# A new written order of one core's instruction queues up to the fifth token group, in a kernel of local attention and a softplus feed-forward layer

## The chip, the cores and the metric

The kernel runs on one core of one Trainium2 chip. The metric is the device time of one execution in microseconds. A core has five engines with a queue each: TensorE (PE; its weight loads are shown as PEld), VectorE (DVE), ScalarE (ACT), GpSimd (POOL) and SyncE (SP, which here only issues transfers). Each queue runs in the order in which it was written, and an instruction that has to wait holds up everything behind it in its queue.

## The reference

Attention over 4 sequences, 8 heads, 768 positions and 64 channels, with a window of the last 96 positions, the first 8 positions for all, and a bias by distance; then two matrix products with a softplus between them.

```python
scores = scale * np.matmul(q, k.transpose(0, 1, 3, 2))
...
scores = scores + bias[None, :, :, :]
scores = np.where(keep, scores, -1000000000.0)
...
a = np.exp(scores)
a = a / (np.sum(a, axis=-1, keepdims=True) + 1e-09)
return np.matmul(a, v).astype(np.float32)
...
h = x @ w_in
g = np.maximum(h, 0.0) + np.log1p(np.exp(-np.abs(h)))
return (g @ w_out).astype(np.float32)
```

x is the attention's output as 3072 tokens of 512 channels; w_in is 512 x 2048, w_out 2048 x 512.

## The kernel before, in words

The tokens are worked in 24 blocks of 128 (`blocks`, line 286), two blocks to a unit (12 units, `UNITS`, line 147) and two to a group of the feed-forward layer (12 groups). Every piece of work is an operation with a name, made by `op` (line 28) with what it reads and writes; `ORDER` (lines 68 to 145) lists the names of all 1045 operations with the engine of each (P, V, A, G, S), and `in_order` (line 56) emits them in that order, so the order of every queue is written out by hand. An operation that can run on several engines (its `alts`) runs on the one that `ORDER` names. The waits follow from what each operation reads and writes. The numbers in a name are the group, block or unit, then the part.

Attention, for unit i or block n:

- `ldq`, `ldk`, `ldv` (line 569): transfers of q, k, v of a unit from DRAM into one of 14 raw tiles, issued by SP (`ldq0.0` and `ldq0.1` by ACT). From unit 3 on they also wait for a given product of the feed-forward layer (`gates`, line 1337).
- `castq`, `castk`, `castv` (lines 650, 682, 690): to bf16.
- `trq`, `trk`: transposes, for units 0 to 2 on PE (line 777) with the evictions `cpq`, `cpk` on DVE or ACT, from unit 3 on by DMA, issued by SP (line 823).
- `gk`, `gv` (lines 846, 862): copies of the 8 global positions into the neighbour block's keys and values.
- `sc` (line 918; `sb` puts the bias into PSUM for blocks 0 and 1), `z` (line 978, adds the bias on DVE), `ex` (line 987, the exponential on ACT), `pv` (line 1009), `nm` (line 1021, reciprocal and multiply on DVE).
- `xt` (line 1023): the transposed attention output into the tile XT; for blocks 0 to 5 on PE with the eviction `xc`, from block 6 on by DMA, issued by SP. The row `PE x_ps L1002` is pv, `s_ps L950` sc, `XT<-xs` xt.

Feed-forward layer, for group g:

- `win`, `wout` (line 617): eight transfers of 512 KB each for w_in and for w_out, cast by `cin` and `cout` (line 644).
- `a{g}.{p}` (line 1069): eight matmuls (row `h_ps L1060`) into one of two PSUM banks; needs both blocks' XT and two slices of w_in. `e` (line 1081) is the exponential on ACT, `ln` (line 1093) the logarithm over two `e`.
- Groups 0 and 1: `b{g}.{ns}.{x}` (line 1122), two matmuls of 512 columns each (row L1107), as the slices of w_out come in; `oc` and `st` (line 1126) copy and store.
- Groups 2 to 11: the second product in the form with seven instead of eight block products. `ws` (line 396) makes sums of w_out's blocks, `ka` (line 438) those of the activations, `b{g}.{j}` (line 525) the products (row L522), `oe` the sums into the output tile, `st` the stores (line 550).

`fill` are matmuls on a zero tile at the start. `iota`, `dl`, `d0`, `bias`, `ident`, `ident_q`, `ident_p`, `ones`, `table` (lines 1148 to 1230) make the constants; `table` loads ACT's function table (line 344). `castk3.0`, for example, is unit 3's k, and `pv5.1` block 5's second half of the heads.

What sets the order around the change: the first units' q, k and v, then w_in, then w_out come through SP's one queue; the products of groups 0 and 1 are interleaved with them slice by slice; in between, the attention of blocks 4 to 9 makes the XT tiles for groups 2 to 4. `pv` of blocks 4 and later writes the bank x_ps, so each needs the `nm` of the one before.

Of the kernel before, what the change touches and what calls it, by code (L numbers as in the profile page):

```python
# [73 lines left out]
win0:S castq0.1:V fill15:P fill16:P win1:S cpq0.0:V trq0.1:P cpk0.0:V castk0.1:A cpq0.1:V sc0.0:P biasTrue5:A
ident_p:V sb1.0:P biasTrue6:V ex0.0:A win3:S trk0.1:P sb1.1:P ex0.1:A cpk0.1:V castk1.0:V sc1.1:P win2:S castq1.1:V
sc1.0:P ex1.1:A castq1.0:V fill17:P castk1.1:G fill18:P fill19:P pv0.0:P fill20:P ex1.0:A nm0.0:V fill21:P castv0.11:G
trk1.0:P ldq2.0:S fill22:P castv1.11:G cpk1.1:V pv0.1:P pv1.1:P nm0.1:V trq1.0:P cpk1.0:A ldq2.1:S castv1.00:G
fill23:P nm1.1:V cpq1.0:A xt0:P ldk2.1:S pv1.0:P castv1.01:A fill24:P cpq1.1:V fill25:P win5:S fill26:P cin0:G nm1.0:V
xc0:A win4:S sc2.0:P xt1:P z2.0:V win6:S fill27:P castk2.0:G xc1:A fill28:P z2.1:V sc3.0:P gk4:A gv4.1:G ex2.0:A
fill29:P cin1:V sc3.1:P castv1.10:A win7:S pv2.0:P fill30:P z3.0:V cin3:G ex2.1:A fill31:P a0.1:P wout0:S nm2.0:V  # L80
a0.0:P ex3.0:A cin2:V wout1:S pv2.1:P fill32:P e0.0:A nm2.1:V fill33:P fill34:P wout2:S castq2.0:A z3.1:V a0.2:P
castq2.1:A ldv2:S e0.1:A xt2:P castk2.1:G trq2.0:P xc2:V ex3.1:A wout3:S gv4.0:G trk2.0:P cpq2.1:V a0.3:P cin5:G
cpq2.0:A cpk2.0:V cpk2.1:V e0.2:A pv3.0:P e0.3:A cin4:G sc4.0:P nm3.0:V ln0.0:A z4.1:V pv3.1:P gk5:G a0.5:P ln0.1:A
# [1305 lines left out]
```

## Time and profile before

| | |
|---|---|
| three runs | 210.63, 210.78, 211.83 us (median 210.78) |
| the profiled execution | 210.41 us, of it the span from first to last instruction 208.6 us |
| granted TensorE clock | 1.0 over the whole span |
| busy in the span | PE 200.5, PEld 164.2, DVE 160.1, ACT 169.2, POOL 114.1 us |
| from HBM, to HBM | 27.26 MB, 6.29 MB |

In the profile's lines, L and a number is a line of the kernel. A line of the timeline has the start and the duration in us, the engine (SPq is a transfer that SP issues), the line, the operation, out<-in by the names of the tiles, shapes, the count of merged instructions, and in brackets the idle time of the engine before it with what ended it. Ends of matmuls are modelled: consecutive ones overlap, so the time that one holds PE is read from start to start. A few matmul records are missing. The chain of work that ended last is given as start, duration, and what. A table of stretches gives, for each, the busy time of every engine and in brackets the instructions, then the granted clock, the busy share of the DMA engines, and GB/s.

### The profile page before, as it was taken

The numbers are of one execution on the slowest core, as the hardware profiler recorded it, in microseconds if no ns is written. First come the engines' busy times: TensorE is split into PE (matmuls) and PEld (weight loads), VectorE is DVE, ScalarE is ACT, GpSimd is POOL, SyncE is SP. The second block draws the span as 40 slices with busy tenths as digits, with TensorE's granted clock in tenths as the row PEclk, the third lists the DMA queues.
The fourth block names the chain that finished last, engine by engine and source line by source line (L and its number), as shares of the span: only waits on it lengthen the run. The fifth ranks groups of instructions, "written<-read, shape, count | busy, mean of one in ns | idle before, by whom it ended". The sixth has DMA issues, their size and how long they took to land.

```text
span 208.6 us, 5507 instructions
## 1 busy us (share of the span) xinstructions
PE 200.5 (96%) x2202; PEld 164.2 (79%) x2211; DVE 160.1 (77%) x297; ACT 169.2 (81%) x246; POOL 114.1 (55%) x120
## 2 busy tenths in 40 slices
...
GB/s 176 364 361 388 387 358 361 335 227 255 210 218 282 187 207 286 191 236 300 195 191 259 209 194 214 159 133 126 104 75 54 100 5 138 66 0 0 104 21 181
DMA packets 70649, 40.99 MB, mean 196 GB/s; under 512 B 30432, under 2 KB 62688, under 8 KB 70624
## 3 DMA queue, kind: packets, MB, share of 16 engines
...
q10 hardware_dynamic: 688, 0.66, 1.0%
...
HBM read 27.26 MB, written 6.29 MB: 161 GB/s over the span
## 4 chain that ended last, share of the span: by engine, by line
PE 73%; DMA 14%; DVE 4%; ACT 2%; POOL 2%; issue 1%; SPq 1%; ACTq 0%; POOLq 0%; DVEq 0%
PE h_ps L1060 35%; PE o_ps L522 25%; DMA raw<-in_q_dram 7%; DMA raw<-in_moe_w_in_dram 5%; PE x_ps L1002 4%; PE s_ps L950 4%; DMA XT<-xs 2%; PE x_ps L522 2%; PE s_ps L1107 2%; PE s_ps L522 1%; POOL vb L868 1%; SPq L640 1%; DVE z L976 1%; POOL qb L675 1%; ACT g L1086 1%
## 5 line engine op out<-in xcount | busy, mean ns | idle before, releaser
L1060 PE MATMUL h_ps<-XT,w_in_bf 128*128 128x256 bf16 x768 | 94.8, 273 | 2.1 <-DMA XT<-xs 1.2
L1060 PEld LDWEIGHTS <-w_in_bf 128*128 128x128 bf16 x768 | 73.2, 98 | 13.4 <-DMA XT<-xs 1.4
L1075 ACT ACTIVATE e<-h_ps 128x512 f32<-128x512 f32 x96 | 60.0, 637 | 16.8 <-PE h_ps L1060 16.1
L1086 ACT ACTIVATE g<-e 128x1024 bf16<-128x1024 f32 x48 | 49.5, 1051 | 0.4
L976 DVE TENSOR_TENSOR z<-s_ps,biasA 128x1024 f32<-128x1024 f32 x38 | 45.9, 1218 | 4.0 <-PE s_ps L950 2.7
L983 ACT ACTIVATE pb<-z 128x1024 bf16<-128x1024 f32 (+1 forms) x44 | 43.5, 992 | 2.4 <-DVE z L976 1.7
L452 POOL TENSOR_TENSOR g<-g 128x1024 bf16<-128x1024 bf16 x12 | 26.0, 2168 | 23.1 <-DVE raw L452 22.9
L522 PEld LDWEIGHTS <-g 128*128 128x128 bf16 x320 | 30.8, 98 | 3.6
L452 POOL TENSOR_TENSOR raw<-g 128x1024 bf16<-128x1024 bf16 x9 | 19.9, 2214 | 15.2 <-ACT g L1086 13.6
L522 PEld LDWEIGHTS <-raw 128*128 128x128 bf16 x240 | 22.5, 98 | 2.8
L522 PE MATMUL o_ps<-raw,raw 128*128 128x256 bf16 x192 | 24.3, 273 | 0.0
L452 DVE TENSOR_TENSOR raw<-g 128x1024 bf16<-128x1024 bf16 x21 | 17.3, 833 | 6.7 <-ACT g L1086 4.2
L522 PE MATMUL o_ps<-raw,g 128*128 128x256 bf16 x160 | 19.7, 273 | 0.0
L868 POOL COPY vb<-vb 4x512 bf16<-4x512 bf16 x22 | 15.2, 692 | 6.8 <-PE x_ps L1002 6.0
L1002 PEld LDWEIGHTS <-pb 128*128 128x128 bf16 x352 | 16.4, 98 | 3.0 <-issue 0.3
L1014 DVE TENSOR_TENSOR xs<-x_ps,rcp 128x256 bf16<-128x256 f32 x40 | 17.0, 425 | 1.4
L707 POOL CAST vb<-raw 64x512 bf16<-64x512 f32 x26 | 16.5, 640 | 2.7 <-DMA raw<-in_v_dram 1.5
L1002 PE MATMUL x_ps<-vb,pb 128*128 128x65 bf16 x304 | 15.8, 193 | 0.1
L522 PE MATMUL o_ps<-w_out_bf,g 128*128 128x256 bf16 x128 | 15.8, 273 | 0.0
L1013 DVE RECIPROCAL rcp<-x_ps 128x4 f32<-128x4 f32 x40 | 7.1, 178 | 7.2 <-PE x_ps L1002 6.5
L1234 PE MATMUL x_ps<-blank 128*128 128x512 bf16 x32 | 11.0, 454 | 1.5 <-DVE blank L1159 1.2
L675 POOL CAST qb<-raw 128x1024 bf16<-128x1024 f32 x7 | 8.1, 1152 | 7.4 <-DMA raw<-in_q_dram 7.1
...
## 6 DMA issues: line engine op xcount, KB each, us to landing
...
```

What stands on the lines that cost most here:

```text
L452: (nc.vector if eng == "DVE" else nc.gpsimd).tensor_tensor(dst, a[0], b[0], ALU.subtract)
L522: nc.tensor.matmul(psum(j), lhs[:, f // 2, f % 2, :], w(f), start=(f == 0 and not (chain and j in "267")), stop=(f == 7), skip_group_check ...
L707: copy_on[eng](dst, src)
L868: copy_on[eng](vb_of(prev)[sl, :, 0:D], vb_of(first)[sl, :, 0:D])
L976: nc.vector.tensor_tensor(z, src, bias, ALU.add)
L983: nc.scalar.activation(pb[:, 0:nr, :].rearrange("p (y a) b -> p y (a b)", y=2), src, AF.Exp, scale=1.0 / root_d)
L1002: nc.tensor.matmul(xv[:, h, :], pb[:, 4 * (h % 2) + 2 * part + h // 2 if lone else u_all * (2 * (h % 2) + h // 2) + u, :], vb_of(prev if u ...
L1014: nc.vector.tensor_tensor(xs[:, 4 * part : 4 * part + 4, :], xv[:, :, 0:D], rcp[:][:, :, None].to_broadcast([P, 4, D]), ALU.mult,)
L1060: last = nc.tensor.matmul(hv[:, j, :], w_in_bf[:, m, fb * P : fb * P + P], XT[g % NXG][:, m, :], start=(m == 0), stop=(m == NM - 1),)
L1075: nc.scalar.activation(e[:, p % 2, :, :].rearrange("p j (b t r) -> p (j b) r t", b=2, r=2), hb[:].rearrange("p (a r t) -> p a r t", a=4, r=2),
L1086: nc.scalar.activation(gt[:, 2 * p - 2 : 2 * p + 2, :].rearrange("p a t -> p (a t)"), e[:].rearrange("p a j t -> p (a j t)"), AF.Ln, bias=1.0,
L1234: nc.tensor.matmul(x_ps[:], blank[:, 0:P], blank[:])
```

## The change

Only `ORDER` changes. The same 1045 operations are there; 82 of them have another engine: 20 go from ACT to DVE, 17 from POOL to DVE, 16 from DVE to POOL, 16 from DVE to ACT, 8 from POOL to ACT and 5 from ACT to POOL. The last 277 entries of the list are as before, and so are the last 155 of PE's 324 entries (from b3.3 on), 114 of DVE's, 123 of ACT's, 50 of POOL's and 52 of SP's. Core of the diff:

```diff
 ENGINES = {"P": "PE", "V": "DVE", "A": "ACT", "G": "POOL", "S": "SP"}
 ORDER = """
-ldv0:S iota:G ldq0.0:A blank:V fill0:P ldk0.0:S ldq0.1:A dl0a:V fill1:P dl0b:V ldk0.1:S fill2:P table:A dl0c:V dl1a:V
-fill3:P fill4:P ldk1.0:S fill5:P d0:G d0e:V fill6:P ldq1.0:S fill7:P dl1c:V biasFalse4:G biasFalse1:A ldq1.1:S fill8:P
...
-cin6:G z4.0:V a0.4:P e0.5:A cin7:G nm3.1:V wout4:S ex4.0:A sc5.0:P xt3:P gv8.0:G a0.7:P e0.4:A z5.1:V cout0:G wout5:S
-xc3:A a0.6:P e0.7:A z5.0:V cout1:G ex4.1:A a1.1:P ldq3:S ws0.4:V ldk3:S e0.6:A b0.0.0:P cout2:G gk6:A b0.1.0:P ws0.3:V
-e1.1:A a1.0:P ex5.0:A a1.3:P castv2.11:V ln0.2:A wout7:S ws0.1:V b0.0.2:P ws0.6:V b0.1.2:P e1.0:A b0.0.4:P castv2.01:V
-castv2.00:A cout3:V a1.2:P ln1.0:A cout4:G pv4.0:P b0.1.4:P e1.2:A nm4.0:V b0.0.6:P ln0.3:A gk8:G ws1.3:V b0.1.6:P
-wout6:S pv4.1:P e1.3:A ldv3:S a1.4:P nm4.1:V gv5.1:G ws1.6:V b0.0.8:P e1.4:A xt4:P ws1.4:V b1.0.0:P gv5.0:A cout5:V
-b1.0.2:P ex5.1:A a1.5:P ws0.7:V xc4:A castv2.10:V b0.1.8:P castq3.0:V ln1.1:A b0.1.10:P ws1.7:V b0.0.10:P trq3:S
-cout7:G e1.5:A pv5.0:P a1.6:P castk3.0:A nm5.0:V ldq4:S ws2.3:V b1.0.4:P e1.6:A trk3.0:S pv5.1:P b1.0.6:P cout6:A
...
-e2.2:A ldk5:S pv6.1:P a2.4:P nm6.1:V gv7.0:G ex7.0:A gv7.1:V castv4.00:G xt6:S b1.1.0:P z7.1:V e2.3:A b1.1.2:P e2.4:A
-b1.1.4:P castv3.11:V trk4.1:S a2.5:P ex7.1:A castq5.0:V pv7.0:P ln2.0:A b1.1.6:P st0.0.0:S nm7.0:V sc8.0:P trq5:S
-ws3.4:V ln2.1:A castk5.0:G pv7.1:P a2.6:P nm7.1:V e2.5:A z8.0:V xt7:S b1.1.8:P gk9:A ws3.3:G e2.6:A b1.1.10:P ln2.2:A
...
+ldv0:S iota:G table:A ldq0.0:A blank:V fill0:P ldk0.0:S ldq0.1:A ones:G dl0a:V fill1:P dl0b:V ldk0.1:S ident:G dl1a:V
+fill2:P dl0c:V dl1c:V fill3:P d0:G fill4:P d0e:V ldk1.0:S fill5:P dl1e:V biasFalse7:G fill6:P ldq1.0:S biasTrue2:V
...
+z4.0:V a0.5:P cin7:G a0.4:P wout6:S nm3.1:V e0.5:A z4.1:V gk5:A xt3:P ex4.0:A cout0:G a0.7:P wout7:S xc3:V e0.4:A
+wout5:S sc5.0:P ws0.6:V e0.7:A ldq3:S a0.6:P z5.1:V cout1:A ldk3:S a1.1:P gk6:V e0.6:A gv8.1:V cout2:V b0.1.0:P
+ln0.2:A a1.0:P ws0.3:V e1.1:A castv2.01:G z5.0:V b0.1.2:P castv2.00:A a1.3:P e1.0:A ws0.4:V castv2.10:A pv4.0:P ldv3:S
+ws0.7:V b0.0.0:P e1.3:A b0.1.4:P nm4.0:V ex4.1:A a1.2:P ws1.4:V cout3:V b0.0.2:P e1.2:A pv4.1:P a1.5:P ln0.3:A nm4.1:V
+ws1.1:V b0.0.4:P ln1.1:A b0.0.6:P ws0.1:V a1.4:P e1.5:A cout4:V ex5.0:A ws1.7:V xt4:P b0.0.8:P cout5:V b0.1.6:P
+ln1.0:A a1.7:P ws1.3:V cout6:V cout7:A ldk4:S b0.1.8:P castv2.11:V b0.0.10:P xc4:V castq3.0:A b0.1.10:P gv5.1:V
+gv8.0:V b0.0.12:P ws2.1:V gv5.0:A b1.0.0:P trq3:S ws2.7:V ex5.1:A b1.0.2:P pv5.0:P castk3.0:V b0.0.14:P e1.4:A ws2.3:V
+b1.0.4:P trk3.0:S castv3.10:G b0.1.12:P ln1.2:A nm5.0:V b0.1.14:P castv3.00:V ws2.4:G pv5.1:P ldq4:S a1.6:P nm5.1:V
...
+ex6.1:A nm6.0:V a2.3:P ldv4:S z7.0:V ldk5:S pv6.1:P e2.3:A b1.1.0:P gv7.0:G a2.4:P nm6.1:V ex7.0:A castq5.0:G z7.1:V
+a2.5:P ln2.1:A gv7.1:G trq5:S b1.1.2:P e2.4:A pv7.0:P sc8.0:P e2.5:A nm7.0:V xt6:S castv4.01:G b1.1.4:P ex7.1:A z8.0:V
+b1.1.6:P castv4.00:G b1.1.8:P ln2.0:A gk9:G castv4.11:V pv7.1:P a2.7:P nm7.1:V castk5.0:G ex8.0:A z8.1:V a2.6:P xt7:S
...
```

The queues that result, in the stretch that matters, old and then new.

PE, from a0.5 to group 3's first product:

```
a0.5 a0.4 sc5.0 xt3 a0.7 a0.6 a1.1 b0.0.0 b0.1.0 a1.0 a1.3 b0.0.2 b0.1.2 b0.0.4 a1.2 pv4.0 b0.1.4 b0.0.6 b0.1.6 pv4.1 a1.4 b0.0.8 xt4 b1.0.0 b1.0.2 a1.5 b0.1.8 b0.1.10 b0.0.10 pv5.0 a1.6 b1.0.4 pv5.1 b1.0.6 a1.7 xt5 b0.0.12 b0.1.12 b0.1.14 b0.0.14 a2.0 b1.0.8 b1.0.10 sc6.0 b1.0.12 b1.0.14 a2.1 a2.2 pv6.0 sc7.0 a2.3 pv6.1 a2.4 b1.1.0 b1.1.2 b1.1.4 a2.5 pv7.0 b1.1.6 sc8.0 pv7.1 a2.6 b1.1.8 b1.1.10 b1.1.12 a2.7 b1.1.14 sc9.0 a3.0

a0.5 a0.4 xt3 a0.7 sc5.0 a0.6 a1.1 b0.1.0 a1.0 b0.1.2 a1.3 pv4.0 b0.0.0 b0.1.4 a1.2 b0.0.2 pv4.1 a1.5 b0.0.4 b0.0.6 a1.4 xt4 b0.0.8 b0.1.6 a1.7 b0.1.8 b0.0.10 b0.1.10 b0.0.12 b1.0.0 b1.0.2 pv5.0 b0.0.14 b1.0.4 b0.1.12 b0.1.14 pv5.1 a1.6 xt5 b1.0.6 b1.0.8 a2.0 sc6.0 a2.1 b1.0.10 b1.0.12 a2.2 b1.0.14 pv6.0 sc7.0 a2.3 pv6.1 b1.1.0 a2.4 a2.5 b1.1.2 pv7.0 sc8.0 b1.1.4 b1.1.6 b1.1.8 pv7.1 a2.7 a2.6 pv8.0 b1.1.10 sc9.0 b1.1.12 b1.1.14 pv8.1 a3.1
```

SP, from the fourth slice of w_out on:

```
wout3 wout4 wout5 ldq3 ldk3 wout7 wout6 ldv3 trq3 ldq4 trk3.0 ldk4 trk3.1 ldv4 trq4 ldq5 trk4.0 ldk5 xt6 trk4.1 st0.0.0 trq5 xt7 st0.1.0 ldv5 ldq6 trk5.0 ldk6 xt8 ldv6 trk5.1 xt9

wout3 wout4 wout6 wout7 wout5 ldq3 ldk3 ldv3 ldk4 trq3 trk3.0 ldq4 trk3.1 ldq5 trk4.1 trk4.0 trq4 ldv4 ldk5 trq5 xt6 xt7 st0.0.0 st0.1.0 ldk6 trk5.0 ldv5 trk5.1 ldv6 ldq6 xt8 xt9
```

DVE, from z5.1 to z6.0:

```
z5.1 z5.0 ws0.4 ws0.3 castv2.11 ws0.1 ws0.6 castv2.01 cout3 nm4.0 ws1.3 nm4.1 ws1.6 ws1.4 cout5 ws0.7 castv2.10 castq3.0 ws1.7 nm5.0 ws2.3 nm5.1 gv6.0 ws2.6 ws1.1 ws2.4 ws3.6 ws2.1 oc0.0.0 ws2.7 z6.0

z5.1 gk6 gv8.1 cout2 ws0.3 z5.0 ws0.4 ws0.7 nm4.0 ws1.4 cout3 nm4.1 ws1.1 ws0.1 cout4 ws1.7 cout5 ws1.3 cout6 castv2.11 xc4 gv5.1 gv8.0 ws2.1 ws2.7 castk3.0 ws2.3 nm5.0 castv3.00 nm5.1 oc0.1.0 xc5 ws2.6 ws1.6 gv6.1 castk4.0 z6.0
```

POOL, from cout0 to castk5.0:

```
cout0 cout1 cout2 cout4 gk8 gv5.1 cout7 castq4.0 gv8.1 castv3.00 gv6.1 castk4.0 ws3.1 gv7.0 castv4.00 castk5.0

cout0 castv2.01 castv3.10 ws2.4 castv3.11 castq4.0 ws3.1 ws3.6 gv7.0 castq5.0 gv7.1 castv4.01 castv4.00 gk9 castk5.0
```

ACT, in the same stretch, now has cout1, castv2.10, cout7, castq3.0, gv6.0 and oc0.0.0, and no longer gk6, xc4, castk3.0, cout6, xc5, oc0.1.0 and castv3.10. POOL's cin5 is now followed by gk8 before cin4.

127 lines of the change are left out of this document (63 added, 64 removed).

## The prediction

> **What bounds the kernel now.** I read the page's busy times first, then stretches of the span, then TensorE's and the other queues' timelines around each place where TensorE stops, and last the chain that ended last. In the page PE is the fullest engine; in the table of stretches (span from 0) its busy time against the length of the stretch tells where it stops.
>
> ```profile
> span 208.6 us, 5507 instructions
> ...
> PE 200.5 (96%) x2202; PEld 164.2 (79%) x2211; DVE 160.1 (77%) x297; ACT 169.2 (81%) x246; POOL 114.1 (55%) x120
> ```
>
> ```profile
> core 0: us, PE busy (x) PEld busy (x) DVE busy (x) ACT busy (x) POOL busy (x), PEclk, DMA share, GB/s
> 0.00:17.30 17.30, 15.52 (x153) 8.46 (x156) 13.35 (x43) 12.21 (x25) 7.46 (x18) 1.00 0.93 309
> 17.30:28.50 11.20, 10.06 (x127) 7.90 (x127) 9.04 (x18) 10.06 (x15) 6.45 (x8) 1.00 1.05 387
> 28.50:50.00 21.50, 21.34 (x190) 14.85 (x192) 20.50 (x35) 20.77 (x33) 8.91 (x11) 1.00 1.08 305
> 50.00:64.74 14.74, 13.26 (x153) 9.51 (x155) 13.76 (x21) 13.38 (x21) 9.54 (x12) 1.00 1.21 223
> 64.74:202.45 137.71, 137.71 (x1562) 121.38 (x1563) 100.60 (x177) 112.83 (x156) 81.76 (x74) 1.00 0.69 148
> ```
>
> From 64.74 us on, when the third group's first product a3.0 begins, PE is busy without a gap, at the full granted clock. So the end is fixed by when a3.0 starts. Up to 28.5 us the DMA engines are full (387 GB/s) and the slices of w_in come one by one: POOL's timeline shows the last four casts (cin5, cin4, cin6, cin7) each waiting for its landing, 1.35 us apart.
>
> ```profile
> 23.47 1.04 POOL L644 CAST w_in_bf<-raw 128x1024 bf16<-128x1024 f32 x1 [0.18 <-DMA raw<-in_moe_w_in_dram]
> 27.53 1.04 POOL L644 CAST w_in_bf<-raw 128x1024 bf16<-128x1024 f32 x1 [0.31 <-DMA raw<-in_moe_w_in_dram]
> ```
>
> PE's timeline gives the other two marks. In the written order its rows are a0.7, a0.6 and a1.1 at 28.57, right behind cin7; then sc6.0 (49.26), a2.5 (56.62), pv7.0 (57.73), b1.1.6 (57.97), sc9.0 (62.88) and a3.0 with a3.1 (64.74).
>
> ```profile
> 28.57 2.86 PE L1060 MATMUL h_ps<-XT,w_in_bf 128*128 128x256 bf16 x24
> ...
> 49.26 0.62 PE L950 MATMUL s_ps<-qT,kT 64*128 64x128 bf16 x16
> ...
> 56.62 1.04 PE L1060 MATMUL h_ps<-XT,w_in_bf 128*128 128x256 bf16 x8
> 57.73 0.40 PE L1002 MATMUL x_ps<-vb,pb 128*128 128x65 bf16 x8
> 57.97 0.59 PE L1107 MATMUL o_ps<-w_out_bf,g 128*128 128x512 bf16 x2
> ...
> 62.88 0.62 PE L950 MATMUL s_ps<-qT,kT 64*128 64x128 bf16 x16
> 64.74 1.92 PE L1060 MATMUL h_ps<-XT,w_in_bf 128*128 128x256 bf16 x16 [1.24 <-DMA XT<-xs]
> ```
>
> How long an operation holds PE is read from the chain, which counts from one start to the next: 0.87 for an a, 0.43 for a b of two matmuls (1.29 for three), 0.24 for a pv, 0.55 for a wide sc, and on DVE 1.13 for a z; for an xt I take 0.22 (four of the same 0.055).
>
> ```profile
> 21.30 1.13 DVE z L976
> ...
> 34.04 1.29 PE s_ps L1107 x6
> ...
> 60.53 4.17 DMA XT<-xs
> 64.74 1.92 PE h_ps L1060 x16
> 66.66 0.24 PE x_ps L1002 x8
> 66.90 0.87 PE o_ps L522 x8
> ...
> 72.87 0.55 PE s_ps L950 x16
> ```
>
> From a0.7 (28.57) to a3.0 (64.74) are 36.17 us. The written order has there 18 a (two of group 0, eight each of 1 and 2), 32 small b, 8 pv, 2 xt and 4 wide sc: 18 x 0.8725 + 32 x 0.43 + 8 x 0.24 + 2 x 0.22 + 4 x 0.555 = 34.05. So PE waits 2.1 us in all there. The largest piece is before a3.0: sc9.0 is done at 62.88 + 0.55 = 63.43, a3.0 comes 1.3 later, when xt7's transposed tile lands. Another is 0.24 before pv7.0 (56.62 + 0.87 = 57.49 against 57.73); pv7.0 waits for castv3.11, which DVE's queue reaches only at 57.25 (its timeline).
>
> ```profile
> 57.25 0.43 DVE L707 CAST vb<-raw 64x512 bf16<-64x512 f32 x1
> ```
>
> **The change part by part.** No operation is added or removed; 82 change their engine, and every queue is reordered up to about the fourth group's work; the last 155 of PE's 324 entries stand as before.
>
> *The start.* ACT's table load comes ahead of the two ldq0 issues, which costs them between 0 and its 1.3 us; castk0.1, castq1.0, castq1.1 and ident_p go to POOL, four evictions (cpq0.0, cpk0.1, cpq1.1, cpk1.1) to ACT, one (cpq1.0) back to DVE. Worked down by hand with the rows' durations, block 1's transposed tile is late by 0 to 1 us.
>
> ```profile
> L344 ACT ACT_TABLE_LOAD x1 | 1.3, 1283 | 2.1 <-issue 2.1
> 20.05 0.69 DVE L644 CAST w_in_bf<-raw 128x1024 bf16<-128x1024 f32 x1 [0.99 <-DMA raw<-in_moe_w_in_dram]
> ```
>
> The cover is the transfer of the fourth w_in slice: cin2 cannot start before 20.05, on DVE before and on ACT now (about 1.02 instead of 0.69), so the second pair of products starts at 21.1 instead of 20.8. That 0.3, and the 0.2 that gk8 between cin5 and cin4 adds, are hidden again by cin7's landing. Value 0; without that cover, up to 1 us.
>
> *At cin7.* Before, sc5.0 ran ahead of a0.7, in the time that PE would have waited for cin7. Now it stands behind a0.7. Likewise pv8.0 and pv8.1 now stand ahead of group 3's first product. So between a0.7 and that product lie 34.05 + 0.555 + 0.48 = 35.09 us of work, of which the 0.48 was to be done later anyway. If no wait at all were left, group 3 would start at 28.57 + 35.09 = 63.66, worth 63.18 in the old order: 1.55 us are to be had (2.1 less sc5.0), not more. What is given back:
>
> *DVE between z5.1 and nm5.0.* DVE now has all of cout2 to cout6 (cout3 and cout5 were its own), castk3.0, gv8.0, gv8.1, gv5.1, xc4 and gk6, and has given castq3.0, castv2.01, castv2.10, ws2.4 and ws3.6 away. In the old order DVE was busy for 20.50 of the 21.50 us in that stretch. Its rows (and one of POOL's) give 0.60 from start to start for a weight sum, and I take the same for a cast of that size, when POOL is still; an nm holds it for 0.56 (42.90 to 43.46).
>
> ```profile
> 42.90 0.18 DVE L1013 RECIPROCAL rcp<-x_ps 128x4 f32<-128x4 f32 x1
> ...
> 43.46 0.82 DVE L417 TENSOR_TENSOR raw<-raw,raw 128x512 bf16<-128x512 f32 x1
> ...
> 46.95 0.67 DVE L417 TENSOR_TENSOR raw<-raw 128x512 bf16<-128x512 f32 x1
> 47.55 0.67 DVE L417 TENSOR_TENSOR raw<-raw,raw 128x512 bf16<-128x512 f32 x1
> ...
> 48.75 1.12 DVE L417 TENSOR_TENSOR raw<-raw 128x512 bf16<-128x512 f32 x1
> ```
>
> ```profile
> 48.29 1.04 POOL L675 CAST qb<-raw 128x1024 bf16<-128x1024 f32 x1 [4.55 <-DMA raw<-in_q_dram]
> ```
>
> sc5.0 ends at 28.57 + 0.87 + 0.56 = 30.0. Behind it DVE has 2 z (1.13), 11 ws, 5 casts and castk3.0 (17 x 0.60), 2 nm (0.56) and six small copies (1.7, an estimate from the 0.43 of the cast above): 15.3, so nm5.0 begins at 45.3 and ends at 45.9, or 46.3 where nm4.1 and cout5 wait for pv4.1 and their slice. PE reaches pv5.1, which needs the bank that nm5.0 frees, after 9 a, 19 b, 3 pv, xt4 and sc5.0, 17.5 us, at 46.1. With castv3.10 and ws2.4 on POOL at that moment it is worse, since the row at 48.75 shows a weight sum of 1.12 instead of 0.67 beside a POOL cast. I take 0.4 (0 to 1.2).
>
> The Trainium skill says why, in its page "GPSIMD Engine Reference", section "1. Specifications": POOL's SBUF interfaces are shared with VectorE, and they contend when DVE runs a two-port mode or has two SBUF inputs. The rows at 48.29 and 48.75 agree. It speaks against this change, which puts five POOL operations beside five such DVE ones; by it the wait is nearer its upper end, and the total 0.8 later than with the lower one.
>
> *SP's queue.* wout6, wout7 and wout5 now go ahead of ldq3 and ldk3, and ldk4 ahead of trq3. While the DMA engines are full, a later place is a later landing: two 512 KB slices, 1.35 each, so ldq3 and ldk3 land some 2.7 later.
>
> ```profile
> 33.90 3.98 SPq L640 DMA_DIRECT2D raw<-in_moe_w_out_dram  x2
> ...
> 42.27 1.34 SPq L837 DMA_TRANSPOSE qT<-qb  x1
> ...
> 44.33 1.38 SPq L830 DMA_TRANSPOSE kT<-kb  x1
> ```
>
> ```profile
> 42.89 1.02 ACT L687 CAST kb<-raw 128x1024 bf16<-128x1024 f32 x1
> ```
>
> ```profile
> kT<-kb SPq DMA_TRANSPOSE x8, 4.9
> ```
>
> castk3.0 on DVE ends about 45.2 (before: 43.9, on ACT), trk3.0 is issued then instead of at 44.33, and its tile lands by the listing of DMA issues 4.9 us later in the middle (at most 4.9 for this one, as sc6.0 at 49.26 needs it): 49.5 to 50.3. PE comes to sc6.0 after 11 a, 21 b, 4 pv, 2 xt and sc5.0, 20.6 us, at 49.2 plus the wait above. I take 0.3 (0 to 0.9).
>
> *Before group 3.* castv3.11 is on POOL, early, so the 0.24 before pv7.0 goes. xt7 needs nm7.1, which needs pv7.1. In the new order pv7.1 ends 4.07 us of PE work ahead of a3.1 (two a, two pv, three b, sc9.0). The chain is nm7.1 with its queue (0.75) and a transpose through DMA. The view of the XT tile gives 2.4 to 5.1 for that, 3.6 in the middle.
>
> ```profile
> DMA to landing us min/median/max: 2.4/3.6/5.1
> ```
>
> With 0.2 for issue the chain is 4.5 against 4.07 of cover: 0.45 of the old 1.3 stays (0 to 1.2, the upper end with the 4.17 of the old xt7). castq5.0 on POOL and trq5 stand ahead of xt7 on SP; by the rows they end about 58, ahead of nm7.1 at 60.9, and cost nothing unless 2 us late.
>
> *Group 4's first product.* nm9.1 now stands behind z10.0 and z10.1 on DVE; 2.4 us behind sc10.0 instead of directly behind pv9.1, so xt9 is some 0.4 later against the same products. I take 0.2 (0 to 1.0).
>
> **The sum.** -1.55 + 0.4 + 0.3 + 0.45 + 0.2 = -0.2. The profiled execution took 210.41 (span 208.6 and 1.8 around it), so it would be 210.2. The runs shown have a median of 210.78, 0.37 over the profiled one; I put half of that on top and predict 210.4.
>
> **The rivals.** *All waits go.* Nothing comes in place of the old ones: 210.41 - 1.55 = 208.9. For it: each of the four waits has 0 as its lower end. Against: all four would have to be at it, and xt7's needs a transpose faster than the middle one.
>
> *The w_in slices land earlier.* POOL's cast at 18.80 waited 1.96 for its slice, while later slices come every 1.35; had that one come on the same step, all landings behind it would be up to 1.5 us earlier, and the mark at 28.57 with them: 210.2 - 1.5 = 208.7; with some of the other waits gone too, 208.6. ldq2.0, which waited for castv0.11 in the old order, is free sooner now. Against: seven transfers were still outstanding then, so the queue was not empty.
>
> ```profile
> 18.80 1.04 POOL L644 CAST w_in_bf<-raw 128x1024 bf16<-128x1024 f32 x1 [1.96 <-DMA raw<-in_moe_w_in_dram]
> ```
>
> *Slower: DVE's queue becomes the bound from 30 to 50 us.* Its five operations beside POOL's at 45 to 48 (ws2.1, ws2.7, castk3.0, ws2.3, castv3.00) each take up to 0.45 more (1.12 against 0.67), 2 us in all. Then pv5.1 waits 1.6, trk3.0 goes out 1.4 later and sc6.0 waits 1.0, and castk4.0, trk4.0 and trq4 behind them make sc8.0 and xt7 late by 1.2 each: -1.55 + 5.0 = +3.4, 213.8 at worst, about 213.0 with two thirds of it. It decides once nm5.0 ends more than 1.5 us behind PE's arrival at pv5.1, that is after 47.6. For it: DVE has no slack there. Against: POOL's rows in that stretch sum to 8.91 of 21.50, most of them not beside these.
>
> **How the numbers follow.** The likeliest, waits that move, gets 0.66; all waits gone 0.12; slices earlier 0.06; DVE the bound 0.16. A measurement of this kernel can tell about 1% (2.1 us) from no change. The likeliest lies within it with its own range (209.0 to 212.0), and so does nearly half of "all gone", whose 208.9 is at the edge. So faster by over 1% gets 0.12, within 1% 0.72, slower 0.16. The range runs from the slices' 208.6 to 212.6, which leaves out the upper part of "DVE the bound".
>
> **What would show it.** Right: a0.7 within 0.4 of 28.57, right behind cin7; pv7.0 without a wait of its own; PE's largest gap still before group 3's first a, ended by an XT transpose, but under 1.3; a gap at pv5.1 ended by DVE's multiply. PE gapless afterwards up to group 4, and its last part as before. Wrong: a0.7 over 1 us from there (the start is not hidden), gaps over 1 us between 30 and 50, or a new gap after 70.

## The result and the profile after

The changed kernel takes 212.35 us (median of 10 runs, 211.86 to 213.34), the kernel before beside it 211.11 (10 runs): a ratio of 1.0065 (95%: 1.0045 to 1.0086). Measured again later on another chip it was 1.0092 (1.0073 to 1.0111). So it is 1.2 to 1.8 us slower, where 0.4 us faster was forecast: inside the range and within the 1%, but on the other side. The profiled execution took 212.53. Of e17, below, only two of six executions ran at a granted clock of 0.999 (the others at 0.983 to 0.992), and only those two times are used; its trace is of one of the others, with a clock of 1.00 up to 54.5 us.

The page of the changed kernel, and the table of stretches for it, cut at a0.7, a2.0, group 3's first product (now a3.1) and a4.0 (at their first weight loads):

```profile
span 210.7 us, 5495 instructions
...
PE 201.0 (95%) x2203; PEld 164.3 (78%) x2211; DVE 159.7 (76%) x300; ACT 170.4 (81%) x246; POOL 108.7 (52%) x117
```

```profile
29.06:49.36 20.30, 19.81 (x179) 13.68 (x180) 19.65 (x40) 19.54 (x28) 5.39 (x5) 1.00 1.03 291
49.36:66.75 17.39, 15.98 (x197) 11.67 (x198) 15.16 (x25) 16.47 (x23) 11.15 (x15) 1.00 1.09 197
66.75:80.86 14.11, 13.62 (x160) 11.67 (x161) 12.15 (x19) 11.55 (x20) 8.83 (x9) 1.00 1.19 228
```

The same table of before, cut at the same products:

```profile
28.52:47.22 18.70, 18.54 (x161) 13.10 (x162) 17.73 (x31) 18.00 (x28) 7.24 (x9) 1.00 1.09 312
47.22:64.74 17.52, 16.04 (x183) 11.24 (x185) 16.54 (x25) 16.12 (x26) 11.19 (x13) 1.00 1.19 229
64.74:78.38 13.64, 13.64 (x168) 12.03 (x169) 11.01 (x22) 12.38 (x18) 9.17 (x10) 1.00 1.08 222
```

PE's busy time counts overlapped ends, so the lengths of the stretches are what to compare, and the two orders put different products into them. The work moved is taken out with the durations of the prediction: in the first stretch the new order does sc5.0 (0.555) and one small b (0.43) more, in the second one b less and pv8.0 and pv8.1 (0.48) more, in the third those two less and pv10.0 (0.24) more. What is left is waiting:

| stretch | before | after | waits added | forecast |
|---|---|---|---|---|
| up to a0.7 | 28.52 | 29.06 | +0.54 | 0 |
| a0.7 to a2.0 | 18.70 | 20.30 | +0.61 | +0.4 (pv5.1) |
| a2.0 to group 3 | 17.52 | 17.39 | -0.18 | -1.35 |
| group 3 to a4.0 | 13.64 | 14.11 | +0.71 | +0.2 |
| sum of the waits | | | +1.68 | -0.75 |

With sc5.0's 0.555 and pv10.0's 0.24 that makes the 2.48 by which a4.0 comes later (80.86 against 78.38). Weight loads run a little ahead of their matmuls (pv8.1's start at 64.88, its matmuls at 65.09). Cut at the matmuls' own starts, the four rows are +0.54, +0.56, -0.11 and +0.81, together 1.80, and a4.0 comes 2.59 later; the single waits below are read from matmul to matmul. The forecast's -1.35 is its 2.1 of old waits less the 0.3 at sc6.0 and the 0.45 before a3.1. Behind a4.0 nothing more is lost: PE's last product starts 2.34 later than before (PE's order is the same from a4.6 on). This is one traced execution of each kernel, 2.12 apart in time; the medians are only 1.2 to 1.8 apart.

Where the waits sit, in the timeline of the changed kernel. At the start (a line is start, duration, engine, line, operation), first the one row of before, the eviction xc1 that finishes block 1's tile:

```profile
15.67 0.59 ACT L1038 COPY XT<-o_ps 128x512 bf16<-128x512 bf16 x1 [0.24 <-PE o_ps L1033]
```

```profile
16.33 0.60 ACT L817 COPY kTa<-s_ps 128x512 bf16<-128x512 bf16 x1
...
17.04 0.41 PE L950 MATMUL s_ps<-qT,kTa 64*128 64x128 bf16 x8 [0.59 <-ACT kTa L817]
...
18.04 0.39 PE L1033 MATMUL o_ps<-ident,xs 128*128 128x128 bf16 x4
...
18.46 0.59 ACT L1038 COPY XT<-o_ps 128x512 bf16<-128x512 bf16 x1 [1.54 <-PE o_ps L1033]
...
21.20 1.04 ACT L644 CAST w_in_bf<-raw 128x1024 bf16<-128x1024 f32 x1
...
22.29 0.94 PE L1060 MATMUL h_ps<-XT,w_in_bf 128*128 128x256 bf16 x7 [0.50 <-ACT w_in_bf L644]
```

sc2.0 (17.04) waits for cpk1.1, an eviction that ACT now reaches only at 16.33; xt1 stands behind it, so block 1's tile is done at 19.05 (before: 16.25). cin2 starts at 21.20, not when its slice lands (20.15), since e0.1 and ex2.1 stand ahead of it on ACT and wait for a0.1. From there PE is behind: a0.7 comes after a0.5, a0.4 and xt3, not right behind cin7 (28.70).

In the second stretch DVE runs without a gap from z5.1 (30.83) to nm5.0, and pv5.1 waits 0.49 for it:

```profile
45.41 0.68 DVE L687 CAST kb<-raw 128x1024 bf16<-128x1024 f32 x1
45.42 1.74 POOL L707 CAST vb<-raw 64x512 bf16<-64x512 f32 x1 [11.21 <-DMA raw<-in_v_dram]
...
46.01 0.67 DVE L417 TENSOR_TENSOR raw<-raw,raw 128x512 bf16<-128x512 f32 x1
...
46.81 0.42 DVE L1014 TENSOR_TENSOR xs<-x_ps,rcp 128x256 bf16<-128x256 f32 x1
...
47.29 0.40 PE L1002 MATMUL x_ps<-vb,pb 128*128 128x65 bf16 x8 [0.33 <-DVE xs L1014]
```

Before group 3:

```profile
56.39 0.57 SPq L609 DMA_DIRECT2D raw<-in_v_dram  x1
...
57.91 3.17 SPq L837 DMA_TRANSPOSE qT<-qb  x1
...
60.91 0.41 PE L1002 MATMUL x_ps<-vb,pb 128*128 128x65 bf16 x8
...
61.18 2.53 SPq L1045 DMA_TRANSPOSE XT<-xs  x2
61.23 0.43 DVE L707 CAST vb<-raw 64x512 bf16<-64x512 f32 x1 [0.30 <-DMA raw<-in_v_dram]
...
61.68 0.18 DVE L1013 RECIPROCAL rcp<-x_ps 128x4 f32<-128x4 f32 x1
61.90 0.42 DVE L1014 TENSOR_TENSOR xs<-x_ps,rcp 128x256 bf16<-128x256 f32 x1
...
65.09 0.41 PE L1002 MATMUL x_ps<-vb,pb 128*128 128x65 bf16 x8
...
66.76 1.48 PE L1060 MATMUL h_ps<-XT,w_in_bf 128*128 128x256 bf16 x12 [1.26 <-DMA XT<-xs]
```

ldv4 is issued at 56.39 (before: 48.37), castv4.11 waits for it on DVE until 61.20, and nm7.1 (61.68 to 62.33) stands behind castv4.11. xt7 is sent at 62.49 and lands at 66.71, 4.2 later. From pv8.1's start (65.09) to a3.1's (66.76) are 1.67, 1.43 of them a wait (before, behind sc9.0: 1.31).

And in group 3, castv5.00 waits on ACT for ldv5 (sent at 68.44, before at 63.03), and e3.5 and e3.4 stand behind it. They empty the two banks that a3.7 and a3.6 write, so PE waits 0.23 at a3.7 (76.00) and 0.57 at a3.6 (77.45):

```profile
68.44 0.56 SPq L609 DMA_DIRECT2D raw<-in_v_dram  x1
...
73.86 0.62 ACT L707 CAST vb<-raw 64x512 bf16<-64x512 f32 x1 [1.02 <-DMA raw<-in_v_dram]
...
75.35 0.60 ACT L1075 ACTIVATE e<-h_ps 128x512 f32<-128x512 f32 x1
...
76.00 1.03 PE L1060 MATMUL h_ps<-XT,w_in_bf 128*128 128x256 bf16 x8
...
76.79 0.61 ACT L1075 ACTIVATE e<-h_ps 128x512 f32<-128x512 f32 x1
...
77.45 1.03 PE L1060 MATMUL h_ps<-XT,w_in_bf 128*128 128x256 bf16 x8 [0.41 <-ACT e L1075]
```

Before, castv5.00 stood behind e3.5 and e3.4 and did not wait:

```profile
71.95 1.35 ACT L1075 ACTIVATE e<-h_ps 128x512 f32<-128x512 f32 x2
73.18 0.60 ACT L707 CAST vb<-raw 64x512 bf16<-64x512 f32 x1
```

xt9 lands at 80.34 in the changed kernel, 0.6 ahead of a4.0's matmuls, so a4.0 has no wait of its own.

### The profile page after: what moved, and what is told of

Its sections match the earlier page's. It is cut to its first block, busy times and chain, and to the rows that moved or that the text cites. A ratio compares the mean times of both kernels' runs of the same rounds, so it can differ in the third digit from the quotient of the medians.

```text
span 210.7 us, 5495 instructions
## 1 busy us (share of the span) xinstructions
PE 201.0 (95%) x2203; PEld 164.3 (78%) x2211; DVE 159.7 (76%) x300; ACT 170.4 (81%) x246; POOL 108.7 (52%) x117
## 4 chain that ended last, share of the span: by engine, by line
PE 69%; DVE 8%; DMA 7%; POOL 5%; ACT 5%; issue 3%; SPq 1%; POOLq 0%; DVEq 0%
PE h_ps L1060 31%; PE o_ps L522 24%; PE s_ps L950 4%; PE x_ps L1002 3%; POOL raw L417 3%; DMA raw<-in_v_dram 3%; DMA raw<-in_k_dram 3%; DMA raw<-in_q_dram 2%; DVE raw L417 2%; PE x_ps L522 2%; PE s_ps L522 1%; ACT pb L983 1%; PE s_ps L1107 1%; ACT g L1086 1%; ACT e L1075 1%
## 5 line engine op out<-in xcount | busy, mean ns | idle before, releaser
L452 POOL TENSOR_TENSOR g<-g 128x1024 bf16<-128x1024 bf16 x11 | 23.9, 2172 | 24.5 <-DVE raw L452 21.3
L707 POOL CAST vb<-raw 64x512 bf16<-64x512 f32 x25 | 18.2, 729 | 19.9 <-DMA raw<-in_v_dram 18.9
L452 POOL TENSOR_TENSOR raw<-g 128x1024 bf16<-128x1024 bf16 x8 | 17.5, 2187 | 16.4 <-ACT g L1086 13.8
L1002 PE MATMUL x_ps<-vb,pb 128*128 128x65 bf16 x304 | 15.8, 193 | 0.3 <-DVE xs L1014 0.3
L522 PE MATMUL o_ps<-w_out_bf,g 128*128 128x256 bf16 x128 | 15.8, 273 | 0.0
L868 POOL COPY vb<-vb 4x512 bf16<-4x512 bf16 x18 | 11.5, 640 | 6.6 <-PE x_ps L1002 6.0
L675 POOL CAST qb<-raw 128x1024 bf16<-128x1024 f32 (+1 forms) x9 | 9.3, 1031 | 6.5 <-DMA raw<-in_q_dram 6.3
L1234 PE MATMUL x_ps<-blank 128*128 128x512 bf16 x33 | 10.5, 438 | 1.3 <-DVE blank L1159 1.2
```

The lines of the kernel that those rows point to most:

```text
L452: (nc.vector if eng == "DVE" else nc.gpsimd).tensor_tensor(dst, a[0], b[0], ALU.subtract)
L522: nc.tensor.matmul(psum(j), lhs[:, f // 2, f % 2, :], w(f), start=(f == 0 and not (chain and j in "267")), stop=(f == 7), skip_group_check ...
L707: copy_on[eng](dst, src)
L868: copy_on[eng](vb_of(prev)[sl, :, 0:D], vb_of(first)[sl, :, 0:D])
L1002: nc.tensor.matmul(xv[:, h, :], pb[:, 4 * (h % 2) + 2 * part + h // 2 if lone else u_all * (2 * (h % 2) + h // 2) + u, :], vb_of(prev if u ...
```

## The experiments

All kernels ran beside the kernel before on the same chip; "+1.20" is the difference of the two medians in us, and in brackets stands the interval of the ratio. The changed kernel itself was +1.24 the first time and +1.81 (e5) the second; a0.7 lies between 28.73 and 29.10 in nine traces of the new start, and between 28.24 and 28.59 in nine of the old one, so 0.44 later in the mean (28.88 against 28.44).

**Start or rest: e1, e2, e5, e7.** The list is cut at a0.7: one order up to there, the other for what remains.

```diff
 e1: -changed order up to sc5.0        +order of before up to a0.7
 e2: -order of before up to a0.7       +changed order up to sc5.0, then before's
 e7: e1, and  -ws0.6:V e0.7:A ldq3:S a0.6:P z5.1:V   +z5.1:V ws0.6:V e0.7:A ldq3:S a0.6:P
```

> The list of before up to a0.7 (with its engines), then the remaining operations in the changed kernel's order. Theory 1 (the start is the larger loss: block 1's transposed tile comes 2.8 us later, 19.05 against 16.25, cin2 on ACT ends at 22.24 instead of 20.75 on DVE, and a0.7 comes 0.54 later with sc5.0's 0.555 still to do): 1.1 us go, so 212.35 - 1.1 = 211.2, a0.7 back at 28.5. Rival (theory 2: the start's lateness is taken up again behind 30 us, and the loss is made around group 3 and group 4): no change, 212.3.

> The opposite half: the changed kernel's list up to sc5.0 behind a0.7, then the remaining operations in the order of before. Theory 1: 211.1 + 1.1 = 212.2, with the old 1.3 before a3.0 made smaller where TensorE comes later to it, down to 211.5. Theory 2: 211.1, as before.

e1: +1.20 (1.0040 to 1.0091), no gain to be seen; its profiled execution, its fastest, took 211.11. Its trace shows why: a0.7 is back at 28.24, but ws0.6 (1.66 instead of 0.7) ran ahead of z5.1, and b0.1.0 waited for that. e2: +2.59 (1.0109 to 1.0155): the new start in front of the old order costs more than theory 1 said; there b0.0.0 waited 1.24 for z5.0.

> The changed kernel itself once more, beside the three kernels below on the same chip, with a second trace: which of its waits are there in every execution. Theory (losses fixed by the order): the same four, 0.7 at pv5.1, 1.6 before a3.1, 0.8 at sc11.0 and a0.7 at 29 less the jitter of the launch; 1.2 to 1.3 us over the kernel before. Rival (a chance of one execution's transfers): another set of waits, or a difference under 0.7.

> e1_old_start with z5.1 ahead of ws0.6 on DVE. In e1's trace b0.1.0 waited 0.88 until z5.1 (31.63) had emptied its bank, since the weight sum ws0.6 ran ahead of it at 1.67 instead of 0.7. Theory 1 (the start costs the changed kernel 1.1 us): without this new wait the gain shows in the times, 1.1 less than the changed kernel beside it (0.1 to 0.2 over the kernel before). Theory 2 (the start is taken up again): the same as the changed kernel.

e5: +1.81 (1.0073 to 1.0111), with waits at the same places in its trace (0.49 at pv5.1, 1.26 before a3.1, 0.46 at a3.7 and 0.58 at a3.6, a0.7 at 28.89). e7: +1.05 (1.0033 to 1.0068), 0.76 less than e5 beside it, the intervals apart. So the start is part of the loss, with 0.8 of the 1.1 expected; new waits of 0.2 to 0.3 each at a1.0, a1.3 and pv4.1, to which PE now comes sooner, took the rest.

**Which step of the start: e9, e10.**

```diff
 e9:  -sc2.0:P ... xt1:P          +xt1:P sc2.0:P
 e10: -nm2.0:V cin2:A             +cin2:V nm2.0:V
```

> The changed kernel with xt1 ahead of sc2.0 on PE. There xt1 stands behind sc2.0, which waits until 16.93 for cpk1.1 (ACT, behind castk2.0 and cpq1.1), though xt1's own input nm1.0 is done at 16.35. If this is why block 1's transposed tile is late: a0.1 from 18.7 to 18.9 to about 17.6, a0.3 to about 21.5 (then bound by cin2 on ACT), a0.7 to 28.6, some 0.3 earlier. If the late tile doesn't decide, since cin2 on ACT does: a0.3 stays at 22.1 and a0.7 at 28.9.

> The changed kernel with cin2 on DVE, ahead of nm2.0, instead of on ACT behind e0.1 and ex2.1. cin2 then ends about 21.0 instead of 22.2. If cin2 on ACT decides: a0.3 about 21.5 instead of 22.1 and a0.7 at 28.6. If the late tile decides: a0.1 at 18.7 keeps the order behind it late, and a0.7 stays within 0.15 of 28.9.

In e9 block 1's tile is done at 17.20, yet a0.1 comes at 18.46, since sc3.0 ahead of it now waits for z2.0; a0.3 comes at 21.66. In e10 cin2 ends at 20.78 and a0.3 comes at 21.54. Both gain 0.5 to 0.6 at a0.3 (22.11 in e5) and lose most of it again by a0.5 (26.71 and 26.84, from 26.94 in e5), since trq2.0 waits 0.6 and 0.8 for castq2.0: a0.7 at 28.66 and 28.78. Times +1.45 (1.0039 to 1.0083) and +1.29 (1.0047 to 1.0081), not told apart from the changed kernel. Neither step alone makes the start late: behind the late tile and cin2 stand castq2.1 and castq2.0, which the new order has behind z3.1 on DVE (before: on ACT, where castq2.0 ran at 20.73).

**Before group 3: e3, e4, e13.**

```diff
 e3:  -castv4.11:V pv7.1:P a2.7:P nm7.1:V         +pv7.1:P a2.7:P nm7.1:V castv4.11:V
 e4:  -trq5:S ... xt6:S ... xt7:S                 +xt6:S ... xt7:S trq5:S
 e13: -trk4.1:S ... trk4.0:S ... trq4:S ... ldv4:S    +ldv4:S trk4.1:S ... trk4.0:S ... trq4:S
```

> The changed kernel with castv4.11 behind nm7.1 on DVE instead of ahead of it. In the changed kernel's trace castv4.11 waits until 61.20 for ldv4, and nm7.1 runs right behind it, 61.68 to 62.33; pv7.1 was done at 61.19. Theory A (the late ldv4 holds xt7 through DVE's queue): nm7.1 and xt7 0.45 earlier, the wait of 1.64 before a3.1 becomes 1.2, 212.35 - 0.45 = 211.9. Theory B (it is SP's queue, where trq5's issue takes from 57.91 to 61.09 ahead of xt6 and xt7): xt7's issue is free at 62.4 at the earliest, behind xt6, so 212.3.

> The changed kernel with xt6 and xt7 ahead of trq5 on SP. Theory A: xt7 waits for nm7.1 until 62.33 all the same and was issued at 62.49, so it goes out at 62.4 and lands at most 0.2 earlier; 212.2 to 212.35, or slower, if trq5, sent 4 us later, reaches sc10.0 late. Theory B: xt7 lands without trq5 ahead of it in the DMA queues, 2.4 to 3.6 after its issue instead of 4.2: 0.6 to 1.6 less, 210.8 to 211.7.

> The changed kernel with ldv4 ahead of trk4.1 on SP (behind ldq5), instead of behind trq4. Its raw tile is free at 49.9 there, and SP was idle from 49.9 to 51.6. Theory C (the losses at group 3 and group 4 come from ldv4's late place: castv4.11 holds DVE for it, and all transfers behind it, trq5, ldv5, xt8, are sent later): ldv4 lands at 54 to 56 instead of 61.2, nm7.1 0.4 earlier, group 3 0.5 to 0.9 earlier, castv5.00 no longer waits for ldv5, a4.0 13.3 to 13.7 behind a3.1; 0.7 to 1.3 less than the changed kernel, so 0.1 to 0.7 over before. Rival D (TensorE's order decides there: pv8.0 and pv8.1, done before group 3, are missing as cover for the exponentials within it): a3.1 up to 0.5 earlier, a4.0 still 14.1 to 14.5 behind it; 0 to 0.4 less.

e3: nm7.1 starts 0.44 behind pv7.1's start instead of 0.77, and the wait before a3.1 is 0.79 instead of 1.43 and 1.26 (e5), as theory A said. The time doesn't follow: +1.46 (1.0054 to 1.0090). In its trace a4.0 comes 1.2 earlier than in the changed kernel's, and 0.9 of it is lost at a6.0, which waits for xt13. That transfer lands 0.05 to 0.7 ahead of a6.0 in eighteen of the twenty traces, 2.3 to 2.4 ahead in e5 and e9.

```profile
61.03 0.18 DVE L1013 RECIPROCAL rcp<-x_ps 128x4 f32<-128x4 f32 x1 [0.42 <-PE x_ps L1002]
61.25 0.42 DVE L1014 TENSOR_TENSOR xs<-x_ps,rcp 128x256 bf16<-128x256 f32 x1
61.71 0.43 DVE L707 CAST vb<-raw 64x512 bf16<-64x512 f32 x1
...
65.81 0.94 PE L1060 MATMUL h_ps<-XT,w_in_bf 128*128 128x256 bf16 x7 [0.63 <-DMA XT<-xs]
```

e4: xt7 is sent at 61.94 and lands 4.1 later all the same; the wait before a3.1 is 1.01, but trk5.0 now comes late and sc10.0 waits 0.83 for it: +1.89 (1.0065 to 1.0109). Theory B falls. e13: ldv4 lands at 57.20 instead of 61.20, and a3.1 comes no sooner (66.61), because ldv4 now takes its turn ahead of trq4, whose tile lands at 59.77 instead of 58.31, and the wait moves to sc8.0:

```profile
55.69 1.32 SPq L837 DMA_TRANSPOSE qT<-qb  x1
...
59.82 0.23 PE L950 MATMUL s_ps<-qT,kT 64*128 64x128 bf16 x2 [0.96 <-DMA qT<-qb]
```

+1.55 (1.0042 to 1.0086): theory C, that ldv4's place alone makes both losses, falls too.

**Group 3 to group 4: e6, e11, e15.**

```diff
 e6:  -castv5.00:A ... gk11:A      +gk11:A castv5.00:A
 e11: e6, and  -sc10.0:P ... z10.0:V ... z10.1:V ... pv9.1:P ... nm9.1:V   +pv9.1:P sc10.0:P ... nm9.1:V z10.0:V z10.1:V
 e15: -ldk6:S trk5.0:S ldv5:S trk5.1:S ldv6:S ldq6:S xt8:S    +ldv5:S ldk6:S trk5.0:S trk5.1:S xt8:S ldv6:S ldq6:S
```

> The changed kernel with castv5.00 behind gk11 on ACT. There castv5.00 waited on ACT until 73.86 for ldv5, which ACT had been free for since 72.84, and gk11 behind it ended at 77.64, 0.77 later than sc11.0 needed it. Theory (the late ldv5 holds sc11.0 through ACT's queue): the wait at sc11.0 goes, and a4.0 comes 0.3 to 0.8 earlier (xt9 lands at 80.34, 0.5 ahead of it): 0.3 to 0.8 less than the changed kernel beside it. Rival (ACT is simply full there, 170.4 of 210.7): gk11 ends as late as before and nothing changes.

> The changed kernel with castv5.00 behind gk11 on ACT, sc10.0 behind pv9.1 on PE as before, and z10.0 and z10.1 behind nm9.1 on DVE. e6 had taken the wait at sc11.0 away, and 0.57 came back at a4.0, where xt9 lands. If xt9's lateness is that of pv9.1 behind sc10.0, its cover grows by 0.55: a4.0 13.7 behind a3.1 instead of 14.1 to 14.5, and 0.4 to 0.8 less than the changed kernel's 1.8 over before in the last call (so 1.0 to 1.4 over before). If xt9's landing is set by transfers ahead of it on SP (xt8 is sent 3 us late), no change: 1.8.

> The changed kernel with two transfers moved on SP, behind group 3's start: ldv5 ahead of ldk6 and trk5.0 (as before), xt8 ahead of ldv6 and ldq6. In every trace of the new order so far castv5.00 holds ACT for 0.6 to 1.0 until ldv5 lands, and with it ln3.1, e3.5, e3.4 and gk11. Theory E (ldv5's place costs group 4 its time through ACT): ldv5 lands about 69, castv5.00 no longer waits, no gap at a3.6 and sc11.0, a4.0 13.3 to 13.6 behind a3.1 instead of 14.1; 0.5 to 0.9 less than the changed kernel, so 0.6 to 1.1 over before. Rival F (xt9's landing is the floor, as in e6): xt9 lands 4.4 behind nm9.1 all the same, a4.0 13.8 to 14.1; 0 to 0.3 less.

The expectations put a wait at sc11.0, for gk11. That was a misreading: gk11 ended at 77.64 in the changed kernel, and sc11.0 began at 78.41, right behind a3.6; the waits are those of a3.7 and a3.6. e6: these two are gone (gk11 is done 1.1 earlier too), but 0.5 comes back at a4.0 (80.87), which now waits for xt9 (80.77): +2.19 (1.0064 to 1.0115). e11: a4.0 14.2 behind a3.1, +1.74 (1.0057 to 1.0114), no change; without sc10.0 ahead of it a3.5 waits 0.63 for ACT's e3.3. e15: castv5.00 no longer waits, and now sc10.0 waits 0.77 for trk5.0, which ldv5 was put ahead of; xt9 lands 0.8 ahead of a4.0, which comes 14.0 behind a3.1, +2.12 (1.0060 to 1.0132).

```profile
67.15 3.40 SPq L830 DMA_TRANSPOSE kT<-kb  x2
...
72.52 0.60 ACT L707 CAST vb<-raw 64x512 bf16<-64x512 f32 x1
...
72.81 0.62 PE L950 MATMUL s_ps<-qT,kT 64*128 64x128 bf16 x16 [0.60 <-DMA kT<-kb]
```

Three waits (ldv5 through ACT, trk5.0, xt9) lie within 1 us of each other there; whichever is taken away, the next ends last.

**The parts together: e8, e14, e16.** e8 is e7 with castv4.11 behind nm7.1, ws2.3 and ws2.7 behind xc5, ex7.1 ahead of e2.4, pv7.1 ahead of b1.1.8, castv5.00 behind gk11, xt8 ahead of ldv6; e14 is e7 with e13's move; e16 is e7 with e3's and e15's.

> e7_old_start_z5 with castv4.11 behind nm7.1, ws2.3 and ws2.7 behind xc5 on DVE, ex7.1 ahead of e2.4 and pv7.1 ahead of b1.1.8, castv5.00 behind gk11, and xt8 ahead of ldv6 on SP: every wait that the trace of the changed kernel shows is taken on. If the loss is the sum of these waits: 1.1 at the start, 0.6 at pv5.1, 0.9 before a3.1 and 0.3 to 0.7 at sc11.0 go, 2.9 to 3.3 less than the changed kernel, 1.6 to 2.0 below the kernel before. If XT transfers behind 80 us, which land 0.1 to 1.1 ahead of their products in all traces, take the place of the waits, 0.5 to 1.5 less than the changed kernel.

> e7_old_start_z5 with the same move of ldv4. If the two losses add up (the start 0.8 by e7's times, ldv4's place 0.7 to 1.3): 1.5 to 2.1 less than the changed kernel, so level with before within 0.4. If one of them only uncovers the other's wait: no more than 1.0 less than the changed kernel, 0.4 to 0.8 over before.

> e15_ldv5_early with the old start of e7 and castv4.11 behind nm7.1. If the losses add: the start 0.8, castv4.11 0.4, ldv5 0.5 to 0.9, 1.7 to 2.1 less than the changed kernel, within 0.3 of before. If they cover each other: 0.9 or less than the changed kernel, as e8 had.

e8: +0.92 (1.0029 to 1.0062); e14: +1.47 (1.0032 to 1.0082); e16: +0.75 (1.0011 to 1.0047). None gets back to before; the parts don't add. e8 came out as its second expectation had it, 0.9 less than e5. e16 lies 0.5 to 1.1 under the changed kernel's 1.24 and 1.81 of the other chips, where its second expectation had up to 0.9; e14 is 0.7 above the top of its second. e8 shows one case: nm5.0 ended 2.1 earlier than in the changed kernel (45.16) and pv5.1's wait was gone, but the weight sums put behind it held z6.0, and pv6.0 waited 1.0 for ex6.0 instead. DVE has no slack from z5.1 to z6.0; an operation moved within that stretch only changes which product waits.

```profile
47.98 0.72 DVE L417 TENSOR_TENSOR raw<-raw 128x512 bf16<-128x512 f32 x1
...
51.47 2.35 DVE L976 TENSOR_TENSOR z<-s_ps,biasA 128x1024 f32<-128x1024 f32 x2
...
53.84 0.33 PE L1002 MATMUL x_ps<-vb,pb 128*128 128x65 bf16 x5 [0.83 <-ACT pb L983]
```

**Which stretch: e17, e18.** e17 has the order of before up to a2.0 and the changed one behind it; e18 has e7's order up to a2.0 and that of before behind it, so only 30 to 48 us is new.

> The list of before up to a2.0, then the remaining operations in the changed kernel's order: only the part behind 47 us is new. If the loss behind the start lies in the queues from 47 us on (SP sends ldv4, ldk5, ldv5, xt8 late): 0.5 to 1.0 over before, with a wait before a3.1 above 1 and a4.0 over 13.6 behind it. If it lies between 30 and 47 us (DVE, nm5.0): level with before or up to 0.5 below.

> The old start with z5.1 ahead of ws0.6 (as e7), the changed kernel's order up to a2.0, then the order of before: only the part from 30 to 47 us is new. If the loss lies from 47 us on: level with before within 0.3. If it lies between 30 and 47 us: 0.6 to 1.2 over before, with nm5.0's wait of 0.6 at pv5.1 in it.

e18: +1.37 (1.0044 to 1.0100), more than the 0.6 to 1.2 expected, with 0.34 and not 0.6 at pv5.1. Its trace divides it: from a0.7 to a2.0 are 20.10 instead of 18.70, 0.97 of it waits; then sc8.0 waits 1.35. That one comes by SP's queue: wout6, wout7 and wout5 ahead of ldq3 and ldk3 make those two land 2.6 later, and ldq4, put behind trk3.0 and with it behind castk3.0, lands at 51.29 (before: 48.16). So castq4.0 and castk4.0 run late on POOL, and trk4.0, sent at 55.23, lands at 60.24 (before: 57.86):

```profile
51.41 1.04 POOL L675 CAST qb<-raw 128x1024 bf16<-128x1024 f32 x1 [2.91 <-DMA raw<-in_q_dram]
...
53.19 1.04 POOL L687 CAST kb<-raw 128x1024 bf16<-128x1024 f32 x1
...
55.23 1.22 SPq L830 DMA_TRANSPOSE kT<-kb  x1
...
60.29 0.23 PE L950 MATMUL s_ps<-qT,kT 64*128 64x128 bf16 x2 [1.19 <-DMA kT<-kb]
```

The changed kernel does not have this wait, though its ldq4 lands later still (52.10): there castk4.0 runs on DVE (50.87), trk4.0 lands at 56.90, and sc8.0 starts at 59.05 right behind pv7.0. So the 1.35 comes from putting the new stretch in front of the old order, and e18's time is not a share of the changed kernel's loss. What it shows is how far the late loads reach.

e17: 213.40 and 213.60, 2.9 to 3.1 over before, and it tells nothing of the stretch behind 47 us: at its seam DVE got gv8.1, castv3.00, gv6.1 and castk4.0 on top of the weight sums that the order of before has between nm5.1 and z6.0, and pv6.0 waited 3.0 for ex6.0. What the new order behind 47 us does by itself stays open; e7, which has it, is not slower than e18, which has not.

**What of it helps: e12.** Three ideas of the change, put into the order of before:

```diff
-b1.1.4:P castv3.11:V          +ws3.1:G castv3.11:G
-trq5:S ... xt7:S              +xt7:S trq5:S
-a3.0:P ... a3.1:P ... pv8.0:P    +pv8.0:P a3.0:P ... a3.1:P
```

> The kernel before with three of the changed kernel's ideas at group 3 alone: castv3.11 on POOL behind ws3.1, trq5 behind xt7 on SP, pv8.0 ahead of a3.0. In the trace of before pv7.0 waited 0.3 for castv3.11, xt7's issue 0.4 for trq5's, and a3.0 1.3 for xt7. If the gain that the prediction saw there is real: pv7.0 0.3 earlier, xt7 0.6 earlier, 0.24 of pv8.0 done in the wait, 0.6 to 0.9 less than before. If xt7's landing takes its time from the transfers beside it: 0 to 0.3 less.

-0.67: 209.97 against 210.64, ratio 0.9970 (0.9950 to 0.9991), the fastest of all these kernels. pv7.0 no longer waits, xt7 is sent at 59.91, 0.6 earlier, and lands in 3.35 instead of 4.17, 0.9 ahead of a3.0; what is left of the wait is pv8.0's, 0.74, for the exponential ex8.0:

```profile
59.91 1.20 SPq L1045 DMA_TRANSPOSE XT<-xs  x1
...
63.91 0.42 PE L1002 MATMUL x_ps<-vb,pb 128*128 128x65 bf16 x8 [0.68 <-ACT pb L983]
64.16 1.91 PE L1060 MATMUL h_ps<-XT,w_in_bf 128*128 128x256 bf16 x16
```

## Why the prediction was wrong, point by point

Three steps of the sum failed: the start, put at 0; the 1.55 us that were "to be had"; and what was to come or stay before group 3 and group 4. Corrected by the traces, -0.2 + 0.54 (start) + 0.55 (to be had) + 0.1 (pv5.1) - 0.3 (sc6.0) + 1.0 (before group 3) + 0.6 (group 4) = 2.3; measured, a4.0 comes 2.59 - 0.24 (pv10.0) = 2.35 later.

- *What bounds the kernel* held: PE, with waits up to group 3; behind a4.0 the two kernels run alike.
- *"1.55 us are to be had"*: half as much again as there was. Of the 2.1 in the old order, 1.31 before a3.0 and 0.24 before pv7.0 are waits for another engine or a transfer. Another 0.4 is 0.1 ahead of each of the four wide score products, with no wait shown; e12, which has the same four, keeps it. Less sc5.0's 0.555, 1.0 was to be had. e12 takes 0.67 in time.
- *The start, "value 0", hidden by cin2's gate and cin7's landing*: failed. Block 1's tile was 2.8 late, not 0 to 1, a0.7 0.44 late in the mean of the traces and not behind cin7, and it cost 0.8 us by e7 and e5. The table load, by contrast, cost the ldq0 issues nothing: 0.74 and 1.48, as before.
- *sc5.0 behind a0.7, 0.555*: right as work; with PE already late there was no wait left for it to hide in.
- *DVE to nm5.0*: the wait at pv5.1, ended by DVE, was as drawn, 0.49 for 0.4. nm5.0 ended at 47.23 instead of 45.9 to 46.3: z5.1, behind sc5.0, began 0.8 later (30.83 for 30.0), and the 15.3 of work took 15.8. PE came to pv5.1 later too (46.8 for 46.1), so the wait came out near the forecast partly by luck.
- *SP's queue*: that ldq3 and ldk3 land 2.7 later was right (42.03 and 43.72; before 39.34 and 40.97), and the wait at sc6.0 stayed within 0 to 0.9: trk3.0 landed at 48.84, ahead of it. But the step stopped there. The lateness went on to the loads behind, which the sum didn't have: in the changed kernel ldv4 and ldv5 each land 6.6 later than before, and with them come the waits of the next two points.
- *"Before group 3: 0.45 of the old 1.3 stays"*: the largest error, 1.26 to 1.43 stayed. That trq5 ahead of xt7 costs nothing was right for xt7 (e4, 0.1 by the issue). Missed was castv4.11, which DVE has directly ahead of nm7.1 and which the late ldv4 held (0.5; e3 shows it). And I took 3.6 for xt7's transfer, the middle of all, where the row of xt7's own transfer said 4.17; it was 4.2.
- *Group 4, +0.2 by xt9*: the wait named was not the one. In the changed kernel xt9 lands 0.6 ahead of a4.0; the 0.8 comes at a3.7 and a3.6, through castv5.00 on ACT, from ldv5's late place on SP, which the sum didn't have (1.0 in e5). xt9 ends last only once these are gone (e6). The new gap behind 70 us was the sign that I had named for "wrong".
- *The rivals*: "DVE the bound" named DVE from 30 to 50 us as the place, and e8 shows that it has no slack; it put the price on slower operations beside POOL, which in this trace fell on POOL (below), and its condition, nm5.0 after 47.6, wasn't met (47.23). "All waits go" and "slices earlier" fell: a0.7 was later, not earlier.

By the page "GPSIMD Engine Reference" of the Trainium skill, section "1. Specifications", I had POOL's casts slow DVE down. Here castk3.0 and ws2.3 kept their 0.68 and 0.67 beside castv3.10, and it was POOL's cast that took 1.74. In e17 it went the other way: castv3.00 on DVE took 1.48 instead of 0.41, beside a POOL weight sum that had started 0.5 earlier.

```profile
49.16 1.52 DVE L417 TENSOR_TENSOR raw<-raw 128x512 bf16<-128x512 f32 x1
50.11 1.69 POOL L417 TENSOR_TENSOR raw<-raw,raw 128x512 bf16<-128x512 f32 x1
50.61 1.48 DVE L707 CAST vb<-raw 64x512 bf16<-64x512 f32 x1
```

The Trainium skill's page "SBUF — State Buffer", section "Who interferes with whom", says of DVE in a two-port mode and GpSimd (POOL) that the one that issues first holds the shared ports for its whole instruction and the other blocks; both traces agree with that (castk3.0 started at 45.41, castv3.10 at 45.42), and the sentence on which I leaned names no loser.

What is shown by times: the start costs 0.8 us. The waits behind it are read from traces; e3, e6 and e15 each remove the one they aim at, and the time does not follow, because another wait takes its place. What stays open: how much of the 1.05 that e7 still loses belongs to which stretch, and why xt7's transfer takes 4.0 to 4.4 in thirteen traces and 3.3 to 3.95 in seven, e12 among them.
